# An attention-plus-FFN kernel on one core: a small constant loaded first by another queue, and one PSUM copy of each of eight head pairs moved from ScalarE to VectorE

## The chip, the cores and the metric

The kernel runs on one core of one Trainium2 chip. The metric is the device time of one execution in microseconds. Repeated runs of one kernel mostly lie within about 0.6% of each other; an occasional first run is far slower (514.19 us once for the kernel before).

Engine names as in the profile: PE is TensorE, DVE is VectorE, ACT is ScalarE, POOL is GpSimd, SP is SyncE. A number such as L226 is a line of the kernel.

## The reference

Local plus pooled attention, then a gated FFN. Cut to what matters:

```python
# q, k, v: (B=8, H=8, S=576, D=64) float32
q_d, k_d, v_d = [x.reshape(B, H, 144, 4, D).mean(axis=3) for x in (q, k, v)]   # pooled 4:1
out_up    = repeat(softmax(q_d @ k_d.T / 8) @ v_d, 4)          # pooled attention
out_local = softmax(band(q @ k.T / 8, |i-j| < 4)) @ v          # local attention
x   = (out_up + out_local)  -> (4608, 512)
out = (relu(x @ w_gate) * (x @ w_val)) @ w_out                 # -> (4608, 512) float32
```

## The kernel before

Two heads ("a head pair", `hp`) are handled together. For the first nine pairs, PE transposes and pools q and k by multiplying with an identity and a summing matrix (`eyesum_sb`, 120 columns of the constants). The result lies in three PSUM banks, and each bank is emptied by two copies: a "pooled" one (128x96) and a full one (128x384).

```python
def emit_qkT_pe(hp, b0, b1):                      # L216
    ...
    for n in blocks:                              # 12 blocks x 2 heads = 24 matmuls, L226
        nc.tensor.matmul(out=ps[..., bank, lo:lo+120], lhsT=sv[...], rhs=eyesum_sb, ...)
    act, dve = nc.scalar.copy, nc.vector.tensor_copy
    if hp == 0:
        plan = ((2, 1, act), (2, 0, act), (1, 1, dve), (1, 0, dve), (0, 1, act), (0, 0, dve))
    else:
        plan = ((0, 1, act), (0, 0, act), (1, 1, act), (1, 0, act), (2, 1, dve), (2, 0, dve))
    for i, pooled, copy in plan:                  # bank, pooled?, engine
        ...                                       # pooled copies: L244, full copies: L246
```

`s1` makes scores (L279, L290), exponentials on ACT (L299, L308) and masks them on DVE (L302). `s2` multiplies by v (L324, L333); DVE then normalises (`rd` L341, `xo` L342, `ru` L349, `xo` L351), and PE transposes the result back (`x`, L460/L464).

```python
def emit_fill(hp):                                # four rounds, before the FFN starts
    emit_in(hp + 4); emit_s1(hp, 2); emit_vd(hp, 6); emit_warm(3 if hp == 0 else 2)
    if hp >= 1: emit_x_pe(hp - 1, 0)
    if hp < LEAD - 1: emit_qkT_pe(hp + 1, 2, 3)
    else: emit_warm(3)
    emit_s2(hp, 6, 0); emit_warm(1)
...
def emit_slot(s, gate):                           # then 36 slots: FFN plus one head pair each
    if NVP <= hp + 1 < NP:
        emit_vd_pool(hp + 1)                      # GpSimd: two sums that pool v, L250 and L251
    emit_in(hp + 4)                               # loads, issued by GpSimd
    ...
# [cut]
        emit_in(0)                                # q by SP (cast by ACT), k and v by GpSimd
        nc.sync.dma_start(cst_sb, cst_dr)         # all constants, one transfer
        for hp in range(1, 4): emit_in(hp)
        emit_warm(10)                             # matmuls on zeros: 4.17 us before, 0.42 each
        emit_qkT_pe(0, 2, 3)
        emit_pads()
        emit_warm(4)
        for hp in range(LEAD): emit_fill(hp)
        # [cut]  the slots, then the last stores
```

The softmax here doesn't subtract the row's maximum and nothing guards it: scores larger than these inputs give would overflow.

## Time and profile before

| | before |
|---|---|
| median time, 3 runs (one of them the slow one) | 358.18 us |
| span of the traced execution | 355.9 us |
| PE busy / DVE / ACT / POOL | 98% / 63% / 60% / 53% |
| start of the first L226 | 6.63 us |
| start of the fourth rd | 24.30 us |
| first rden (L399) | 33.80 us |
| last DVE copy to the end of the span | 3.1 us |

From the page of the kernel before: span, busy time and shares of the engines, and (third line) the shares of the chain that ended last.

```profile
span 355.9 us, 7231 instructions
PE 347.7 (98%) x2852; PEld 177.8 (50%) x2852; DVE 225.2 (63%) x336; ACT 212.4 (60%) x366; POOL 189.2 (53%) x233
PE 91%; DVE 4%; ACT 3%; DMA 1%; issue 1%; DVEq 0%; POOLq 0%
```

PE sets the time (98% busy, 91% of the chain that ended last); other engines count only where PE waits. The chain in order of time, kernel before (start in us, length in us, what):

```profile
1.31 5.27 DMA qk_0_75<-in_k_dram
...
16.06 0.39 PE ps L333 x12
16.46 0.18 DVE rd L341
...
26.88 0.47 DVE xT L474
...
33.80 0.77 ACT rden_112 L399
...
71.32 0.76 DVE xT L407
72.08 2.24 DVE ee_103 L302 x2
```

The start waits for the load of k. In the fill, rd follows directly on the end of s2's matmuls. Much later, at 71 to 74 us, PE waits for two DVE lines.

The early DMA issues of the kernel before (queue, count, KB, us from issue to landing):

```profile
cst_sb<-cst SPq DMA_DIRECT2D x1, 342.0 KB, 4.7
qk_0_75<-in_k_dram POOLq DMA_DIRECT2D x1, 144.0 KB, 5.3
```

The constants, issued at 1.20, land at 5.9; k, issued at 1.31, at 6.6. The timeline of the kernel before at the copies of the second round, and at the fourth rd (start, length, engine, line, and in brackets the idle time and its releaser):

```profile
15.82 0.26 DVE L244 CAST qkd_100<-ps 128x96 f16<-128x96 f32 x1
15.99 0.55 DVE L246 CAST qkT_98<-ps 128x384 f16<-128x384 f32 x1
16.02 0.51 ACT L246 CAST qkT_98<-ps 128x384 f16<-128x384 f32 x1
...
23.39 0.41 PE L324 MATMUL ps<-vd_106,ed_105 72*128 72x65 f16 x8
23.75 0.53 PE L333 MATMUL ps<-vw_92,ee_103 112*128 112x65 f16 x12
24.30 0.18 DVE L341 RECIPROCAL rd<-ps 72x4 f32<-72x4 f32 x1 [0.60 <-PE ps L333]
```

ACT's last copy ends at 16.53 and DVE's at 16.54. The fourth rd, which reads only what L324 wrote, starts 0.5 us after L324's end.

### The profile page before, as it was taken

The numbers are of one execution on the slowest core, as the hardware profiler recorded it, in microseconds if no ns is written. First come the engines' busy times: TensorE is split into PE (matmuls) and PEld (weight loads), VectorE is DVE, ScalarE is ACT, GpSimd is POOL, SyncE is SP. The second block draws the span as 40 slices with busy tenths as digits, with TensorE's granted clock in tenths as the row PEclk, the third lists the DMA queues.
The fourth block names the chain that finished last, engine by engine and source line by source line (L and its number), as shares of the span: only waits on it lengthen the run. The fifth ranks groups of instructions, "written<-read, shape, count | busy, mean of one in ns | idle before, by whom it ended". The sixth has DMA issues, their size and how long they took to land.

```text
span 355.9 us, 7231 instructions
## 1 busy us (share of the span) xinstructions
PE 347.7 (98%) x2852; PEld 177.8 (50%) x2852; DVE 225.2 (63%) x336; ACT 212.4 (60%) x366; POOL 189.2 (53%) x233
## 2 busy tenths in 40 slices
PE   6999999999999999999999999999999999999996
PEld 2665555545544555555555555555444444444443
DVE  5894666687786677777787888877665523232220
ACT  3767776676667776666666666666677532322321
POOL 8986557999999877777778877712000000000000
PEclk9999999999999999999999999999999999999999
DMA  9999999999999999999999999940000100000012
GB/s 148 167 171 188 181 195 153 176 164 186 179 158 171 155 130 132 132 129 131 133 135 131 132 120 114 125 106 31 30 20 17 47 38 30 31 29 29 31 58 91
DMA packets 166882, 40.25 MB, mean 113 GB/s; under 512 B 149728, under 2 KB 162240, under 8 KB 166848
## 3 DMA queue, kind: packets, MB, share of 16 engines
q0 software_dynamic: 132960, 22.93, 85.5%
q1 hardware_dynamic: 28688, 7.56, 15.3%
q10 hardware_dynamic: 5200, 9.31, 7.4%
q8 instruction: 22, 0.36, 0.4%
q14 instruction: 12, 0.10, 0.1%
HBM read 46.45 MB, written 9.44 MB: 157 GB/s over the span
## 4 chain that ended last, share of the span: by engine, by line
PE 91%; DVE 4%; ACT 3%; DMA 1%; issue 1%; DVEq 0%; POOLq 0%
PE ps L483 51%; PE ps L510 25%; PE ps L424 3%; PE ps L226 2%; PE ps L290 2%; PE ps L279 2%; PE ps L432 2%; DMA qk_0_75<-in_k_dram 1%; DVE xn_114 L402 1%; PE ps L540 1%; ACT rden_112 L399 1%; DVE ee_103 L302 1%; ACT rden_112 L401 1%; PE ps L363 1%; PE ps L263 0%
## 5 line engine op out<-in xcount | busy, mean ns | idle before, releaser
L483 PE MATMUL ps<-xT,wg_sb 128*128 128x512 f16 x432 | 111.3, 379 | 0.9 <-DVE xn_114 L402 0.5
L483 PE MATMUL ps<-xT,wv_sb 128*128 128x512 f16 x432 | 111.0, 379 | 0.0
L510 PE MATMUL ps<-wo_sb,gT 128*128 128x512 f16 x420 | 100.1, 380 | 0.0
L483 PEld LDWEIGHTS <-wv_sb 128*128 128x128 f16 x432 | 42.1, 98 | 50.8
L483 PEld LDWEIGHTS <-wg_sb 128*128 128x128 f16 x432 | 39.7, 97 | 44.5 <-issue 0.7
L510 PEld LDWEIGHTS <-gT 128*128 128x128 f16 x420 | 39.0, 98 | 45.6
L518 ACT COPY y_sb<-ps 128x512 f32<-128x512 f32 x35 | 20.5, 586 | 46.9 <-PE ps L510 46.9
L448 DVE TENSOR_TENSOR xn_115<-ps,rden_113 64x720 f16<-64x720 f32 x24 | 21.7, 905 | 21.2 <-ACT rden_113 L445 20.8
L448 DVE TENSOR_TENSOR xn_114<-ps,rden_112 64x720 f16<-64x720 f32 x22 | 19.9, 905 | 21.1 <-ACT rden_112 L445 20.7
L299 ACT ACTIVATE ee_102<-ps 112x576 f16<-112x576 f32 x32 | 19.0, 647 | 13.4 <-PE ps L290 12.8
L299 ACT ACTIVATE ee_103<-ps 112x576 f16<-112x576 f32 x32 | 19.0, 647 | 12.5 <-PE ps L290 12.3
L442 ACT ACTIVATE rden_113<-ps 64x720 f32<-64x720 f32 x24 | 18.3, 764 | 6.9 <-PE ps L432 6.7
L302 DVE TENSOR_TENSOR ee_103<-ee_103,cst_sb 112x576 f16<-112x576 f16 x32 | 21.3, 706 | 0.0
L442 ACT ACTIVATE rden_112<-ps 64x720 f32<-64x720 f32 x22 | 16.8, 764 | 6.0 <-PE ps L432 5.7
L302 DVE TENSOR_TENSOR ee_102<-ee_102,cst_sb 112x576 f16<-112x576 f16 x32 | 19.3, 637 | 1.3 <-ACT ee_102 L299 1.1
L579 PE MATMUL ps<-zero_sb 128*128 128x512 f16 x30 | 10.2, 453 | 1.3 <-DVE zero_sb L131 1.3
L407 DVE TENSOR_TENSOR xT<-xn_115 128x576 f16<-128x576 f16 x14 | 11.3, 807 | 0.1
L407 DVE TENSOR_TENSOR xT<-xn_114 128x576 f16<-128x576 f16 x14 | 11.1, 789 | 0.1
L308 ACT ACTIVATE ed_104<-ps 72x576 f16<-72x576 f32 x16 | 10.3, 642 | 0.0
L308 ACT ACTIVATE ed_105<-ps 72x576 f16<-72x576 f32 x16 | 10.3, 642 | 0.0
L445 ACT ACTIVATE rden_113<-rden_113 128x720 f32<-128x720 f32 x12 | 9.6, 804 | 0.4
L251 POOL TENSOR_TENSOR vd_106<-v_0_87 72x256 f16<-72x256 f32 x4 | 2.9, 722 | 12.2 <-PE ps L432 12.2
(464 smaller groups left out, 601.6 us busy)
## 6 DMA issues: line engine op xcount, KB each, us to landing
out_dram<-y_sb ACTq DMA_DIRECT2D x34, 256.0 KB, 3.9
wg_sb<-in_moe_w_gate_dram POOLq DMA_DIRECT2D x4, 384.0 KB, 10.0
wv_sb<-in_moe_w_val_dram POOLq DMA_DIRECT2D x4, 384.0 KB, 10.5
wo_sb<-in_moe_w_out_dram POOLq DMA_DIRECT2D x4, 384.0 KB, 11.9
vw_90<-in_v_dram POOLq DMA_DIRECT2D x5, 168.0 KB, 6.0
vw_91<-in_v_dram POOLq DMA_DIRECT2D x5, 168.0 KB, 6.3
vw_92<-in_v_dram POOLq DMA_DIRECT2D x5, 168.0 KB, 6.5
v_4_86<-in_v_dram POOLq DMA_DIRECT2D x5, 144.0 KB, 6.9
```

Source lines behind the costliest of these rows:

```text
L299: nc.scalar.activation(out=o, in_=ps[0:WK, p0 + 2 * g : p0 + 2 * g + 2, 0:288], func=AF.Exp, scale=scale)
L302: nc.vector.tensor_tensor(out=o, in0=o, in1=_sap(masks_sb, (0, WK), 288 * g, [[0, 2], [1, 288]]), op=ALU.mult,)
L308: nc.scalar.activation(out=ed[r2][:, :, 0 : 2 * SD].rearrange("p h (c t) -> p c h t", c=2), in_=ps[0:72, p0 : p0 + 4, 288:432].rearrange(" ...
L407: nc.vector.tensor_tensor(out=xT[:, kk, b * S : (b + 1) * S].rearrange("p (c t f) -> p c t f", c=2, f=4), in0=x[:, :, 0:288].rearrange("p ...
L424: nc.tensor.matmul(out=ps[:, bank, NQ * j : NQ * j + NQ], lhsT=vflat[:, v0 : v0 + 128], rhs=e[:, hh, lo : lo + NQ], start=True, stop=True,)
L442: nc.scalar.activation(out=r[lo : lo + 64], in_=ps[de : de + 64, 4 + 2 * hh : 6 + 2 * hh, 0:360], func=AF.Ln)
L445: nc.scalar.activation(out=r, in_=r, func=AF.Exp, scale=-1.0)
L448: nc.vector.tensor_tensor(out=x[lo : lo + 64], in0=ps[lo : lo + 64, 4 + 2 * hh : 6 + 2 * hh, 0:360], in1=r[lo : lo + 64], op=ALU.mult,)
L483: nc.tensor.matmul(out=pair(pp)[:, which, :], lhsT=w[:, kk, bass.ts(jj, 128)], rhs=xT[:, kk, c * TCH : (c + 1) * TCH], start=(kk == 0), st ...
L510: nc.tensor.matmul(out=y_ps, lhsT=gts[c, jj][:, bass.ts(ty, 128)], rhs=wo_sb[:, jj, :], start=(jj == 0), stop=(jj == NJJ - 1),)
L518: nc.scalar.copy(out=y_sb, in_=y_ps)
L579: nc.tensor.matmul(out=ps[:, 7, :], lhsT=zero_sb[:, 0:128], rhs=zero_sb[:, 128:640], start=True, stop=True)
```

## The change

The intent: PE's first real matmuls need only 120 of the 1368 constant columns, so these come first, by ScalarE's queue; the rest follows q. One warm-up matmul becomes needless. For head pairs 1 to 8 the pooled copy of bank 1 goes from ACT to DVE, so that ACT, whose last copy s1 waits for (0.24 us in the second round), is done sooner.

```diff
-            plan = ((0, 1, act), (0, 0, act), (1, 1, act), (1, 0, act), (2, 1, dve), (2, 0, dve))
+            plan = ((0, 1, act), (0, 0, act), (1, 1, dve), (2, 1, dve), (2, 0, dve), (1, 0, act))
@@
+        nc.scalar.dma_start(cst_sb[:, 960:1080], cst_dr[:, 960:1080])
         emit_in(0)
-        nc.sync.dma_start(cst_sb, cst_dr)
+        nc.sync.dma_start(cst_sb[:, 0:960], cst_dr[:, 0:960])
+        nc.sync.dma_start(cst_sb[:, 1080:1368], cst_dr[:, 1080:1368])
@@
         emit_pads()
-        emit_warm(4)
+        emit_warm(3)
```

## The prediction

> **What bounds the kernel.** TensorE. The page gives it 98% busy, and the chain of waits that ended last is 91% PE, 4% DVE, 3% ACT, 1% DMA. From about 72 us on, the chain is matmuls almost without a gap (5.18 us per 24 gate/value matmuls). The change can act only in three early places:
>
> 1. Start. In the chain, 1.31 to 6.58 us is one piece: the load of k for head pair 0 (issued 1.31, landing after 5.3 us). Then the 24 transpose/pool matmuls (L226) start at 6.63. By the DMA issue list all constants, one load of 342 KB issued at 1.20, land after 4.7 us, at about 5.9; q lands at about 4.1 and its cast ends at 4.94.
> 2. Fill, 9 to 27 us: four rounds. The chain's loop, 3.97 us, is s2 matmuls, DVE rd/xo (16.46 to 18.22), x matmuls, L226 matmuls, s2. ScalarE is not in it after the first round.
> 3. First slots, 27 to 60 us: the chain is PE, then ACT rden, DVE xn, PE. L226's evacuations are not in it: ACT idles 1.55 to 1.61 us before each rden, DVE 2.9 us before a product.
>
> **Costs.**
> - Identity first: L226 will no longer need the whole constants. But k lands 0.7 us after them, so k still releases L226. [...] the DMA share is full from about 2 us. Masks (first use 9.86), pool (9.23) and rep4 (14.29) keep slack. Gain 0, plus or minus 0.3 us of landing noise.
> - One warm matmul fewer: after L226 four run 7.38 to 8.42, but s1 waits until 8.73 for DVE's qkT copy, whose order is unchanged. Gain 0; the clock stays full.
> - Pooled copy (128x96) for head pairs 1 to 8: ACT loses a 0.26 us copy (0.13 us start to start), DVE gains one (0.26, 0.17 start to start). In rounds 1 and 2 of the fill ACT's last qkT copy ends at 16.53, DVE's at 16.54, and s1's weights wait 0.24 us for ACT's. So ACT is relieved, but DVE's copy ends level with it and s1 needs both: no gain. DVE is busy with the xT copy until 15.75, then copies from 15.82, and rd follows at 16.46, exactly when the s2 matmuls end. The added copy uses the small hole before 15.82 and delays rd by some 0.04 to 0.15 us in each of two rounds, on the chain. In the first round and the slots DVE has idle time (1.02, 0.19, 0.34 us) for it.
>
> Sum: about +0.1 to +0.3 us in the fill, start 0 or slightly less, rest 0: +0.1 us.
>
> **Predicted: 358.3 us, range 357.3 to 359.2.** Faster by over 2%: 0.01; within 2%: 0.98; slower by over 2%: 0.01.
>
> **What would show it.** L226 still released by the k load at 6.3 to 6.9; identity landed well before that. The first s1 matmul 2.1 us after L226 starts, as before. Fill loop 3.97 to 4.15 us with the DVE copies directly before rd. First rden Ln (33.80 before) at 33.5 to 34.2. From there the gaps equal before's.
>
> **What would make it wrong.** L226 really waited for the constants (their landing is later than the list says, or k's landing is set by their big transfer): then L226 starts up to 0.7 us earlier and the kernel gains that, 357.6. L226 made to wait for all three pieces of the constants: up to 0.5 us later. DVE less tight before rd, and s1's wait for ACT really the limit: 0.1 us less per round.

The sum: the fill +0.1 to +0.3, the start 0 or slightly less, the rest 0, together +0.1 us. The 0.3 us of landing noise and the 0.5 us for a wait for all three pieces are estimates, not measured; the first L226 of the traces below starts at 6.22 to 6.79 us, after_cstlate aside.

## The result, and the profile after

The changed kernel took 357.79 us (median of 6 runs, 357.52 to 358.34), the kernel before 358.03 (median of 6 runs of its own, the slow 514.19 among them). The ratio of the fast runs is 0.9998, with a 95% interval of 0.9984 to 1.0012: the same. Ratios here are the mean time of one kernel's fast runs over that of the other's of the same rounds, so they are not quite the ratio of the medians. The traced run of the changed kernel was the slowest of its six (span 356.6 us; the other five 355.7 to 356.5), which matters wherever the two traces are compared below.

The page of the changed kernel:

```profile
span 356.6 us, 7224 instructions
PE 347.2 (97%) x2851; PEld 177.8 (50%) x2851; DVE 227.0 (64%) x344; ACT 211.5 (59%) x358; POOL 189.0 (53%) x233
PE 90%; DVE 4%; ACT 3%; DMA 1%; issue 1%; DVEq 0%; POOLq 0%
```

Eight copies went from ACT to DVE (344 DVE instructions for 336) and PE's work is the same. Its chain in order of time:

```profile
1.30 5.13 DMA qk_0_75<-in_k_dram
...
15.86 0.39 PE ps L333 x12
16.26 0.18 DVE rd L341
...
26.55 0.47 DVE xT L474
...
33.47 0.77 ACT rden_112 L399
...
70.99 2.33 DVE xT L407
73.32 0.91 DVE ee_103 L302
```

At the first rden the changed kernel leads by 0.33 us (33.47 for 33.80). At 71 us one DVE instruction takes 2.33 us where it took 0.76, and the lead is gone. The early DMA issues of the changed kernel:

```profile
qk_0_75<-in_k_dram POOLq DMA_DIRECT2D x1, 144.0 KB, 5.1
cst_sb<-cst SPq DMA_DIRECT2D x1, 240.0 KB, 3.5
cst_sb<-cst SPq DMA_DIRECT2D x1, 72.0 KB, 3.6
cst_sb<-cst ACTq DMA_DIRECT2D x1, 30.0 KB, 2.7
```

The identity, issued at 0.77, is there at about 3.5 us, the other two pieces, issued at 1.20 and 1.84, at about 4.7 and 5.4, and k still lands last, at 6.4. The timeline of the changed kernel at the same two places:

```profile
15.46 0.41 DVE L244 CAST qkd_100<-ps 128x96 f16<-128x96 f32 x2
15.79 0.55 DVE L246 CAST qkT_98<-ps 128x384 f16<-128x384 f32 x1
16.37 0.11 PEld L279 LDWEIGHTS <-qkd_100 64*72 64x72 f16 x2 [0.24 <-DVE qkT_98 L246]
...
23.18 0.41 PE L324 MATMUL ps<-vd_106,ed_105 72*128 72x65 f16 x8
23.54 0.53 PE L333 MATMUL ps<-vw_92,ee_103 112*128 112x65 f16 x12
23.69 0.18 DVE L341 RECIPROCAL rd<-ps 72x4 f32<-72x4 f32 x1 [0.20 <-PE ps L324]
```

The added copy (now two L244 in a row) fits before DVE's full copy. s1's weights still wait 0.24 us, now for DVE's copy in place of ACT's. The fourth rd starts 0.1 us after L324's end and does not wait for L333.

Where PE lost the lead, first in the kernel before, then in the changed one (the timelines at 71 us, DVE and POOL):

```profile
71.32 0.76 DVE L407 TENSOR_TENSOR xT<-xn_114 128x576 f16<-128x576 f16 x1
71.37 1.72 POOL L250 TENSOR_TENSOR v_0_87<-v_0_82 72x512 f32<-72x512 f16 x1
72.00 2.31 DVE L302 TENSOR_TENSOR ee_103<-ee_103,cst_sb 112x576 f16<-112x576 f16 x2
73.16 0.82 POOL L251 TENSOR_TENSOR vd_107<-v_0_87 72x256 f16<-72x256 f32 x1
```

```profile
70.99 2.33 DVE L407 TENSOR_TENSOR xT<-xn_114 128x576 f16<-128x576 f16 x1
71.53 1.16 POOL L250 TENSOR_TENSOR v_0_87<-v_0_82 72x512 f32<-72x512 f16 x1
72.77 1.13 POOL L251 TENSOR_TENSOR vd_107<-v_0_87 72x256 f16<-72x256 f32 x1
73.24 1.34 DVE L302 TENSOR_TENSOR ee_103<-ee_103,cst_sb 112x576 f16<-112x576 f16 x2
74.27 0.29 PE L424 MATMUL ps<-ee_103,vw_91 112*128 112x96 f16 x3 [0.69 <-DVE ee_103 L302]
```

In both kernels some of DVE's instructions here are longer beside GpSimd's sums than without them (in after_late below, L407 takes 0.76 us and the two masks 0.82): in the kernel before the masks take 2.31 us, in the changed one L407 takes 2.33, though it began 0.54 us before the first sum, and the masks 1.34. Not every DVE instruction is longer beside a sum: L407 of the kernel before takes 0.76, and L500 takes 0.67 to 0.69 us and L209 1.34 to 1.35 throughout both traces, with a sum beside it or without. L407 and the masks together take 3.67 us in the changed one, for 3.07. The end differs as well. SP's waits, kernel before and changed kernel (who waited for whom, us, times, longest):

```profile
SPq L696 <- DMA out_dram<-y_sb: 0.9, 1, 0.9
```

```profile
SPq L698 <- DMA out_dram<-y_sb: 1.3, 1, 1.3
```

The account of the two traces, 0.7 us in all: start of L226 -0.16; from there to the first rden -0.17 (33.47 - 6.47 = 27.00 for 33.80 - 6.63 = 27.17); from the first rden to the matmuls of L483 that follow L424 in the sixth slot +0.60 (75.38 - 33.47 = 41.91 for 75.11 - 33.80 = 41.31); from there to the last DVE copy 0.00 (353.07 - 75.38 and 352.80 - 75.11 are both 277.69); and from that copy to the end of the span +0.4 (356.6 - 353.07 for 355.9 - 352.80).

### The profile page after: what moved, and what is told of

The parts are those of the page before. It is cut to its first block, busy times and chain, and to the rows that moved or that the text cites. A ratio compares the mean times of both kernels' runs of the same rounds, so it can differ in the third digit from the quotient of the medians.

```text
span 356.6 us, 7224 instructions
## 1 busy us (share of the span) xinstructions
PE 347.2 (97%) x2851; PEld 177.8 (50%) x2851; DVE 227.0 (64%) x344; ACT 211.5 (59%) x358; POOL 189.0 (53%) x233
## 4 chain that ended last, share of the span: by engine, by line
PE 90%; DVE 4%; ACT 3%; DMA 1%; issue 1%; DVEq 0%; POOLq 0%
PE ps L483 51%; PE ps L510 25%; PE ps L424 3%; PE ps L226 2%; PE ps L290 2%; PE ps L279 2%; PE ps L432 2%; DMA qk_0_75<-in_k_dram 1%; DVE xn_114 L402 1%; PE ps L540 1%; DVE xT L407 1%; ACT rden_112 L399 1%; ACT rden_112 L401 1%; PE ps L363 1%; PE ps L263 0%
## 5 line engine op out<-in xcount | busy, mean ns | idle before, releaser
L483 PE MATMUL ps<-xT,wg_sb 128*128 128x512 f16 x432 | 111.3, 380 | 0.9 <-DVE xn_114 L402 0.5
L483 PE MATMUL ps<-xT,wv_sb 128*128 128x512 f16 x432 | 111.0, 379 | 0.0
L483 PEld LDWEIGHTS <-wv_sb 128*128 128x128 f16 x432 | 42.2, 98 | 50.7
L483 PEld LDWEIGHTS <-wg_sb 128*128 128x128 f16 x432 | 39.8, 97 | 44.4 <-issue 0.7
L302 DVE TENSOR_TENSOR ee_102<-ee_102,cst_sb 112x576 f16<-112x576 f16 x32 | 20.0, 659 | 1.3 <-ACT ee_102 L299 1.1
L302 DVE TENSOR_TENSOR ee_103<-ee_103,cst_sb 112x576 f16<-112x576 f16 x32 | 19.4, 645 | 0.0
L407 DVE TENSOR_TENSOR xT<-xn_114 128x576 f16<-128x576 f16 x14 | 13.3, 948 | 0.1
L579 PE MATMUL ps<-zero_sb 128*128 128x512 f16 x29 | 9.7, 446 | 1.3 <-DVE zero_sb L131 1.3
L407 DVE TENSOR_TENSOR xT<-xn_115 128x576 f16<-128x576 f16 x14 | 10.9, 778 | 0.1
```

The costliest lines, as they stand in the source:

```text
L302: nc.vector.tensor_tensor(out=o, in0=o, in1=_sap(masks_sb, (0, WK), 288 * g, [[0, 2], [1, 288]]), op=ALU.mult,)
L407: nc.vector.tensor_tensor(out=xT[:, kk, b * S : (b + 1) * S].rearrange("p (c t f) -> p c t f", c=2, f=4), in0=x[:, :, 0:288].rearrange("p ...
L483: nc.tensor.matmul(out=pair(pp)[:, which, :], lhsT=w[:, kk, bass.ts(jj, 128)], rhs=xT[:, kk, c * TCH : (c + 1) * TCH], start=(kk == 0), st ...
L579: nc.tensor.matmul(out=ps[:, 7, :], lhsT=zero_sb[:, 0:128], rhs=zero_sb[:, 128:640], start=True, stop=True)
```

## The experiments

Theories on the table after the two traces: the lead comes from (a) the loads, (b) the moved copy, or (c) chance; the loss comes from (a) GpSimd's sums colliding with DVE, or (b) something else in the traffic at 71 us; the longer end comes from (a) the third constant load, or (b) chance. Twelve runs were made, two of them repeats of the two kernels themselves; all gave correct results. Times alone can't resolve tenths of a microsecond here, so the landmarks of the traces decide. "Second L226" is the transposing matmuls of head pair 1; "products" is the start of the 16 gate/value matmuls after L424 in the sixth slot; "end" is from the start of the last DVE copy to the end of the span. All in us; the columns were subtracted from the timelines and chains.

| kernel | first L226 | second L226, after first | fourth rd, after second L226 | first rden, after second | products, after second | end | span |
|---|---|---|---|---|---|---|---|
| before | 6.63 | 4.29 | 13.38 | 22.88 | 64.19 | 3.1 | 355.9 |
| ctl_before | 6.41 | 4.29 | 13.40 | 22.90 | 64.20 | 3.1 | 355.7 |
| changed | 6.47 | 4.29 | 12.93 | 22.71 | 64.62 | 3.5 | 356.6 |
| ctl_after | 6.27 | 4.29 | 12.94 | 22.72 | 64.71 | 3.5 | 356.5 |
| eye_only | 6.48 | 4.30 | 13.39 | 22.89 | 64.22 | 3.5 | 356.2 |
| pool_only_again | 6.53 | 5.55 | 12.94 | 22.72 | 63.61 | 3.2 | 356.6 |
| before_pad3 | 6.79 | 4.29 | 12.98 | 22.75 | 64.07 | 3.2 | 356.0 |
| after_late | 6.24 | 4.30 | 12.94 | 22.72 | 63.62 | 3.5 | 355.6 |
| before_late | 6.39 | 5.55 | 13.39 | 22.89 | 63.79 | 3.2 | 356.6 |
| two_loads_late | 6.22 | 4.29 | 12.94 | 22.72 | 63.61 | 3.1 | 354.9 |
| two_loads_late_warm12 | 6.49 | 4.55 | 12.94 | 22.72 | 63.60 | 3.1 | 355.4 |
| after_cstlate | 5.64 | 5.22 | 13.19 | 23.98 | 64.86 | 3.5 | 357.2 |
| after_twice | 6.68 | 4.69 | 12.95 | 22.73 | 64.87 | 3.5 | 357.4 |

### ctl_before: the kernel before, traced again

No edit.

> The kernel before, unchanged, traced a second time, to learn how far its landmarks move by themselves. Landmarks of the first trace: L226 starts at 6.63 us, fourth reciprocal rd at 24.30, first rden Ln at 33.80, xT sum (L407) of the sixth slot 0.76 us long, gate/value matmuls after the first L424 at 75.11. If the lead of 0.33 us that the changed kernel has at the first rden Ln (33.47) is chance, this trace shows a start of L226 or a fourth rd up to 0.2 to 0.6 us elsewhere; if the change made it, all come back within 0.05 us, except that the load's landing may move.

One run, 357.52 us (state unknown, a single run). All gaps come back within 0.02 us; only the start moved, to 6.41, by more than the 0.16 in question. So the start of the changed kernel at 6.47 shows nothing by itself, and the 0.17 us at the first rden (22.71 for 22.88) is not chance.

### eye_only: the loads alone

```diff
+        nc.scalar.dma_start(cst_sb[:, 960:1080], cst_dr[:, 960:1080])
         emit_in(0)
-        nc.sync.dma_start(cst_sb, cst_dr)
+        nc.sync.dma_start(cst_sb[:, 0:960], cst_dr[:, 0:960])
+        nc.sync.dma_start(cst_sb[:, 1080:1368], cst_dr[:, 1080:1368])
```

> Only the constants' loads are changed. Theory A (the load of k, not the constants, releases L226; order of loads is worth nothing but noise): L226 at 6.4 to 6.7 us, still released by k; after that the same gaps as before, so the fourth rd lags L226 by 17.67 us as before (24.30 minus 6.63) and the first rden Ln by 27.17. Theory B (the earlier identity made the start 0.16 us earlier): L226 at 6.47 again or less. Time ratio to before 1.000 within 0.1%.

Ratio 1.0003 (0.9968 to 1.0037). L226 at 6.48, released by k; all fill gaps as before; but the end is 3.5 us. The loads bring nothing in the fill, and they bring the longer end.

### pool_only and pool_only_again: the moved copy alone

```diff
-            plan = ((0, 1, act), (0, 0, act), (1, 1, act), (1, 0, act), (2, 1, dve), (2, 0, dve))
+            plan = ((0, 1, act), (0, 0, act), (1, 1, dve), (2, 1, dve), (2, 0, dve), (1, 0, act))
```

> Only the pooled copy is moved. Theory A (the added copy fits into the hole before the copy of the last bank, and rd comes earlier because of the new order): fourth rd lags L226 by 17.2 us as in the changed kernel (23.69 minus 6.47), the first rden Ln by 27.0 and not 27.17. Theory B (the lead comes from the loads alone): lags of 17.67 and 27.17 as before. Theory C, that on record (the copy delays rd): lags longer than before by 0.08 to 0.3 us. Time ratio 1.000 within 0.1%.

Ratio 0.9998 (0.9975 to 1.0020) from its three fast runs. The trace fell in a slow state (599.2 us, clock 0.559), so its landmarks tell nothing.

> The moved pooled copy alone, once more, because the trace of its first run fell in a slow state. Theory A (the moved copy is what brings the fourth rd forward): fourth rd 17.2 us after the start of L226, first rden Ln 27.0 us after it, and the end 3.1 us after the last DVE copy as in the kernel before. Theory B (the loads did it): 17.67 and 27.17.

One run, 358.39 us. Against expectation the fourth rd came 18.5 us after the first L226, because PE was slow for longer: the first L226 took 1.41 us and the four L579 behind it 1.89, for 0.82 and 1.04 in the kernel before. This is called the late clock below; that it is the clock is the reading of these lengths (the profile's own record of the granted clock says 1.00 there). The timeline of pool_only_again, PE:

```profile
6.53 1.41 PE L226 MATMUL ps<-cst_sb,qk 96*64 96x120 f16 x24 [0.82 <-DMA qk<-in_k_dram]
7.87 1.46 PE L579 MATMUL ps<-zero_sb 128*128 128x512 f16 x3
```

The same 24 matmuls take 0.82 us in the traces of before and changed, and the second L226 comes 1.26 us late. From there on, the fourth rd (12.94) and the first rden (22.72) are those of the changed kernel. So the moved copy is what brings the lead of 0.17 us. This trace lost nothing at the products (63.61), but its PE was 1.26 us late while GpSimd was not, so it can't say what the moved copy alone does there when L226 takes 0.82 us.

### before_pad3: the same shift in DVE's stream without the copies

```diff
     for t in qkT:
         nc.vector.memset(t[:, 2 * S :], 0.0)
+    for _ in range(3):
+        nc.vector.memset(ones_sb[:, 64:128], 4.0)
```

> The kernel before with three more short memsets on DVE at about 4.7 us, where it is idle; nothing else moves. It shifts the fourth rd by as many places in DVE's instruction stream as the three added copies do. Theory S (rd's late start in the kernel before depends on its place in the stream[...]): fourth rd 17.2 us after L226. Theory C (it depends on the copies themselves and who makes them): 17.67 us as in the kernel before.

One run, 357.73 us. The fourth rd of before_pad3 in its timeline (its line numbers are two higher):

```profile
23.54 0.41 PE L326 MATMUL ps<-vd,ed 72*128 72x65 f16 x8
23.90 0.53 PE L335 MATMUL ps<-vw,ee 112*128 112x65 f16 x12
24.06 0.18 DVE L343 RECIPROCAL rd<-ps 72x4 f32<-72x4 f32 x1 [0.21 <-PE ps L326]
```

Three idle-time memsets at 4.7 us bring the fourth rd from 13.38 to 12.98, and the first rden from 22.88 to 22.75: 0.13 of the 0.17 us. So most of the lead has nothing to do with ACT or DVE being relieved. It goes with the place of rd in DVE's instruction stream, which is three instructions further on in before_pad3 and in the changed kernel than in the kernel before. The other 0.04 us is there at the first rd after the second L226 already: 1.51 to 1.52 us after it in the seven traces with the moved copy whose second L226 took 0.82 us, 1.56 to 1.57 in before_pad3 as in the other traces without it. The built programs ask rd in both kernels to wait for the same last matmul of L324 (and for an ACT copy long done); why it started 0.5 us after it in one place and 0.1 us after it in another no run here shows.

### after_late: the changed kernel with GpSimd's sum elsewhere

```diff
-        if NVP <= hp + 1 < NP:
+        if NVP <= hp + 1 < NP and s != 5:
             emit_vd_pool(hp + 1)
         emit_in(hp + 4)
+        if s == 5:
+            emit_vd_pool(hp + 1)
```

> The changed kernel with one GpSimd sum (of v for the eleventh head pair) put behind the next loads. Theory A (the lead of 0.33 us is lost at 71 us [...]: L407 took 2.33 us instead of 0.76, and the masks 1.34 instead of 0.82): both come back to 0.76 and 0.82, the products after the first L424 start at about 73.2 instead of 75.38, and the kernel is 1 to 2 us (0.3 to 0.6%) faster than before, if the sum does no harm in its new place. Theory B (the long DVE instructions come of something else, such as the DMA traffic or the transposes then): L407 and the masks stay long together, the products start at 75.0 to 75.4, ratio 1.000.

Ratio 0.9990 (0.9972 to 1.0008), less than was expected. The timeline of after_late, DVE:

```profile
70.79 0.76 DVE L407 TENSOR_TENSOR xT<-xn 128x576 f16<-128x576 f16 x1
71.47 0.82 DVE L302 TENSOR_TENSOR ee<-ee,cst_sb 112x576 f16<-112x576 f16 x2
```

With GpSimd's sums at 76 us and later, L407 is back at 0.76 and the masks at 0.82. The products come at 63.62, 1.0 us earlier than in the changed kernel and 0.57 earlier than before. PE is then without a gap there, so the further 0.9 us by which DVE is early are worth nothing; that is why 1 to 2 us was too much. A second witness is after_cstlate below: there GpSimd waited 1.38 us for a load of k and began the sum, left at its place in the program, only at 74.83, after the masks, and L407 and the masks took 0.76 and 0.82 us as well.

### after_twice: GpSimd's first sum done twice

```diff
         nc.gpsimd.tensor_tensor(out=m, in0=t[:, :, 0:128], in1=t[:, :, 128:256], op=ALU.add)
+        if hp == 10:
+            nc.gpsimd.tensor_tensor(out=m, in0=t[:, :, 0:128], in1=t[:, :, 128:256], op=ALU.add)
```

> The changed kernel with GpSimd's first sum for the eleventh head pair done twice, to the same place (1.16 us more of GpSimd). Theory A [...]: L407 and the two masks together take about 1 to 1.2 us more than in the changed kernel (2.33 plus 1.34), and the products after the first L424 start that much later, 69.9 to 70.1 us after L226. Theory B (the DVE instructions are long for another reason): 68.9.

(Theory A, here and in after_late: what it tests is (a) of the loss, the collision.)

One run, 359.19 us. The products came at 64.87 after the second L226, only 0.16 to 0.25 later than in the two traces of the changed kernel, and L407 with the masks took 1.59 + 2.30 = 3.89 us for 2.33 + 1.34 = 3.67. This is a miss: 1 to 1.2 us had been expected. The second sum itself took 1.56 us in place of 1.16. GpSimd's first and last sum in after_twice (line numbers of the last are two higher):

```profile
71.42 1.16 POOL L250 TENSOR_TENSOR v<-v 72x512 f32<-72x512 f16 x1
74.30 0.82 POOL L253 TENSOR_TENSOR vd<-v 72x256 f16<-72x256 f32 x1
```

Most of the miss is explained by GpSimd's start. Here it began 60.05 us after the second L226 (71.42 - 11.37); in the two traces of the changed kernel it began at 60.77 and 61.52, because it had waited 0.75 and 1.08 us for a load of k just before (here 0.27, by the trace for no load). So its last sum ended only 0.61 and 0.15 us later than there (63.75 for 63.14 and 63.60). In all seven traces in which PE waited here, the masks end shortly after GpSimd's last sum (0.31 to 0.33 us in five, 0.68 in changed and eye_only), and the products start 0.80 us after the masks. GpSimd's recorded spans are rough, but what PE loses goes with the moment at which GpSimd ends, not with the length of its sums alone. That the sums delay DVE stands by the runs that move them (L407 0.76 and the masks 0.82 us in after_late and before_late). In this trace PE's granted clock was 0.52 from 7.5 to 9.0 us and 0.50 from 9.0 to 11.0, after 1.67 us of idle before L226, and the second L226 came 4.69 us after the first, not 4.29; what lowered the clock is not shown.

### ctl_after: the changed kernel, traced again

No edit.

> The changed kernel, unaltered, traced a second time. Landmarks of its first trace: L226 at 6.47; from there 17.22 us to the fourth rd, 27.00 to the first rden Ln, 68.91 to the products after the first L424; 3.5 us from the last DVE copy to the end. Theory: 17.2 and 27.0 come back within 0.05 (unless TensorE's clock comes up late, as once seen), 3.5 as well. The 68.91 may move with the collision of GpSimd's sums and DVE: anything between 68.0 and 69.0; if it is 68.3 or less, the loss of the first trace was partly chance. L226 between 6.2 and 6.5 would speak for a small real gain of the identity's own load (four traces with it 6.22 to 6.48, four without 6.41 to 6.79, the one with the constants behind q's cast left out).

One run, 358.25 us. Everything came back, the loss too (64.71). The collision had another shape (L407 0.76, the masks 2.99) for much the same loss.

### before_late: the kernel before with the sum elsewhere

The edit of after_late, made to the kernel before.

> The kernel before with only GpSimd's sum moved behind the next loads. Theory: L407 0.76 and the masks 0.82, products after the first L424 at 68.1 us after L226 (67.92 in the changed kernel with the same move plus the 0.17 that the moved copies bring), end 3.1 us after the last DVE copy. Ratio to before 0.998 to 0.9995.

Ratio 0.9999 (0.9978 to 1.0020); its six runs spread from 356.83 to 359.02. The traced one had the late clock again (L226 1.41 us), and the second L226 came 1.26 us late. From the second L226 the products come at 63.79, 0.40 earlier than before and 0.17 later than in after_late: the part that the moved copies bring, once nothing collides. The time shows none of it, because the 1.26 us are more.

### two_loads_late: after_late with two constant loads, not three

The identity is laid out as the first 120 constant columns, so that the rest is one piece.

```diff
-        nc.scalar.dma_start(cst_sb[:, 960:1080], cst_dr[:, 960:1080])
+        nc.scalar.dma_start(cst_sb[:, 0:120], cst_dr[:, 0:120])
         emit_in(0)
-        nc.sync.dma_start(cst_sb[:, 0:960], cst_dr[:, 0:960])
-        nc.sync.dma_start(cst_sb[:, 1080:1368], cst_dr[:, 1080:1368])
+        nc.sync.dma_start(cst_sb[:, 120:1368], cst_dr[:, 120:1368])
```

> The changed kernel with the GpSimd sum moved as in the run above, and the identity put in front of the other constants so that they are loaded by two transfers and not three. Theory T (the end is 0.4 us longer in the changed kernel [...]): the end comes 3.0 to 3.1 us after the last DVE copy, not 3.5. Rival: it stays 3.5, because the ScalarE transfer or chance made it. Products after L424 start 67.9 us after L226. Time ratio to before 0.997 to 0.999; spans near 355.2 if L226 starts at 6.45.

(Theory T: what it tests is (a), the third load.)

Median 356.59 us, ratio 0.9970 (0.9954 to 0.9987), the fastest of all. SP's wait for the last store in two_loads_late:

```profile
SPq L699 <- DMA out_dram<-y_sb: 0.8, 1, 0.8
```

The end is 3.1 us, as in every kernel without the third constant load (3.1 to 3.2, six traces more) and not 3.5 as in every kernel with it (six traces). It still loads the identity by ScalarE, so that load is not the cause. The traces of before and changed show what the time went to. The last store lands 1.68 us after its issue in both (353.25 to 354.93, 353.52 to 355.20). SP's check for it is recorded at 354.94 in the first and at 355.22 in the second; after it comes one more check in the first (0.06 us), and seven more in the second (0.43 us in all). The 0.37 us between them is most of the 0.4. The two ends, 3.1 and 3.5, fit theory (a). That the third load moved the check is what these two traces suggest; no run moves it and leaves the number of transfers as it is.

### after_cstlate: the other constants out of k's way

```diff
-        nc.sync.dma_start(cst_sb[:, 0:960], cst_dr[:, 0:960])
-        nc.sync.dma_start(cst_sb[:, 1080:1368], cst_dr[:, 1080:1368])
+        nc.scalar.dma_start(cst_sb[:, 0:960], cst_dr[:, 0:960])
+        nc.scalar.dma_start(cst_sb[:, 1080:1368], cst_dr[:, 1080:1368])
```

(ScalarE reaches these behind the cast of q.)

> The changed kernel, with the constants other than the identity issued by ScalarE behind the cast of q, at about 5.0 us[...]. Theory K (k's landing is set by all that the engines move before it): k lands 0.4 to 1 us earlier, L226 starts at 5.5 to 6.1. Rival (k's landing is set by its own descriptors and latency): 6.2 to 6.6 as in all traces so far. The masks and the pool matrix then land at about 8.6; if that is later than 9.1 the first L263 waits for it.

Ratio 1.0003 (0.9981 to 1.0025). L226 starts at 5.64, 0.58 to 1.15 us earlier than in all other traces, and is still released by k. So k came earlier with the constants issued later, as far as one trace shows. But they now landed 5.7 and 5.8 us after issue (3.5 and 3.6 in the changed kernel), L263 waited 0.9 us for them, and at the fifth L226 PE waited for that head pair's k, which landed at 25.9. The gain was given back. The late clock (L226 took 1.41 us) was in this trace, too.

### two_loads_late_warm12: more warm-up

```diff
-        emit_warm(10)
+        emit_warm(12)
```

> The fastest version so far (ratio 0.997) with 12 warm-up matmuls in place of 10 before L226, so that TensorE's idle time there is shorter. Landmarks from L226 as in that version: 17.2 to the fourth rd, 67.9 to the products, 3.1 at the end; L226 at full clock (24 in 0.82 us, not in 1.41 as seen once). Ratio to before 0.996 to 0.998.

Median 357.15 us, ratio 0.9971 (0.9959 to 0.9983). L226 took 1.07 us and not the 0.82 expected, between that and the 1.41 of the late clock. Two more warm-up matmuls brought nothing that these runs show.

## Why the prediction was right or wrong

- **The time and the class** were right: 357.79 us in a range of 357.3 to 359.2, the same within 2%.
- **The load of k, not the constants, releases L226**: right. In all traces k is the releaser. The identity landed 3 us before it. Traces with the small first load started L226 at 6.22 to 6.68 (seven traces), those without at 6.39 to 6.79 (five): some tenth may be in it, but the two overlap. The alternative in the prediction, that k's landing is set by the constants' transfer, was half true: after_cstlate moved it by 0.6 us and more, but by issuing them later, not by splitting them.
- **The warm matmul is worth nothing**: right for its place. s1 follows L226 by 2.10 us in both (8.73 - 6.63, 8.57 - 6.47). PE was no slower after it: the second L226 took 0.82 us in both, and the granted clock reads 1.00 in both up to 12 us. No run takes this matmul out alone.
- **s1 gains nothing, since DVE's copy ends level with ACT's**: right, and visible: the same 0.24 us wait, with another releaser.
- **"The added copy uses the small hole before 15.82 and delays rd by some 0.04 to 0.15 us in each of two rounds"**: wrong. This is the step that failed. The copy fits wholly into the hole (15.46 to 15.62), and no round became longer (the loop, forecast at 3.97 to 4.15 us, took 3.92 and 3.97); the fourth rd came 0.45 us earlier and the first rden 0.17 earlier. before_pad3 shows that 0.13 of the 0.17 comes with the mere place in DVE's stream, which no cost of a copy could have told.
- **"From there the gaps equal before's"**: wrong. The wait at 71 us, already in the chain of before, was read over. There PE waits for DVE, and DVE's masks end 0.31 to 0.68 us after GpSimd's last sum; PE lost 0.43 and 0.52 us net against before in the two traces of the changed kernel (64.62 and 64.71 for 64.19). In the first, GpSimd ended much as in before (63.14 us after the second L226 for 63.06) and DVE ended 0.35 us later behind it; in the second, GpSimd ended 0.54 us later. GpSimd's start differed by 1.5 us among three traces whose programs are the same up to there (60.05 in after_twice; 60.77 in changed and 61.52 in ctl_after, behind waits of 0.75 and 1.08 us for a load of k). An earlier DVE alone did not bring the loss: before_pad3, 0.13 us earlier, kept its lead (64.07). Whether the change itself moves GpSimd, these runs leave open: pool_only_again had the late clock (L226 1.41 us), eye_only lost nothing (64.22).
- **Not in the prediction at all**: the end, 0.4 us, which came with the third constant load (3.1 to 3.2 us with one or two, 3.5 with three).
- By the sum of the terms, +0.1 us was the forecast; the traces give -0.17 (fill), then +0.6 (collision), +0.4 (end) and a start that varies by nearly 0.6 us. That the number came out right is in part luck: these terms were not forecast, and 28 of the 29 runs of the kernel before that were timed beside the experiments lie in the same range, so that a forecast of no effect at all would have done as well. The timed ratio is 0.9998 and not the 1.002 that the two traces suggest. One reason is that the traced run of the changed kernel was the slowest of its six; the 29 runs of the kernel before have spans of 355.0 to 357.0 us, with a mean of 356.2, above the 355.9 of its trace. The fill and the end, which came back in every trace that could show them, sum to about +0.2 us, and that lies inside the interval of the ratio (about -0.6 to +0.4 us). How much the collision costs in runs without a trace, and how often they have the late clock (1.26 us in pool_only_again and before_late), can't be seen.

## What to carry to other kernels

Moving work between two engines pays only where the later of the two is what the bottleneck waits for (here s1 waited 0.24 us for ACT before and 0.24 us for DVE after); read both ends before crediting either. A lead won early can be lost at the next place where one engine delays another (here 0.17 us won by the first rden, 0.60 lost at 71 us), so follow the chain to its end, not to the last changed instruction. When an effect is below half a per cent, compare landmarks in several traces of both kernels, with a control that repeats each, and look where the traced run lies among the timed ones, before believing any part of it.
